# The first four loads of an FNet and SwiGLU kernel, each in two halves of the partitions on two queues

## The chip, the cores and the metric

The kernel runs on one core of a Trainium2 chip. The metric is the device time of one execution in microseconds (us); the kernel before takes 969.46 us, the median of three runs (969.38 to 969.82). A core has TensorE (PE in the profile, with PEld for its weight loads), VectorE (DVE), ScalarE (ACT), GpSimd (POOL) and SyncE (SP), each with an instruction stream of its own, and 16 DMA engines that move data between the chip's main memory and the core's on-chip memory of 128 partitions.

## The reference

`x` has 2048 rows of 640; everything is float32.

```python
xn = _layernorm(x, axis=-1)
# FNet: real part of a DFT over the hidden dim (640) and the sequence (2048)
a = einsum("bsd,ed->bse", xn, dft_hid_re)
b = einsum("bsd,ed->bse", xn, dft_hid_im)
s = einsum("ts,bse->bte", dft_seq_re, a) - einsum("ts,bse->bte", dft_seq_im, b)
# SwiGLU on the same xn
g = silu((silu(xn @ w_gate) * (xn @ w_up)) @ w_down)
return x + s * g
```

## The kernel before

Every float32 product is made of three faster matmuls: an operand is split in a high and a low part (`hl`, by ScalarE and VectorE), and high x high, high x low and low x high are summed in PSUM (`ps`). Products of blocks go by Strassen's seven-product scheme, so VectorE also adds and subtracts blocks. The sequence DFT comes first: for each of four passes `seq(k)` the matrices `cs` (the real and imaginary DFT matrices, cut in 128 x 1024 pieces) are the moving operand and rows of the normalised `x` the weights. Then `hid_s` (hidden DFT), `gate_up` and `down` follow.

All work is recorded first and ordered afterwards. A step of the code calls `pl.prod` (something that has to be ready by a time), `pl.step` (matmuls) or `pl.post`; `schedule` gives each a time, and the list is played back in the order of these times, each operation on its engine's stream. So one line (L82, the recorder) stands in the profile for nearly everything, and the tiles' names tell operations apart: `xn` is `x` and its normalised rows, `raw` any float32 buffer (pieces of `cs` among them), `hl` split operands, `bst`, `mv`, `sm` and `rowst` the statistics of the layer norm.

The change lies in `opening()` (L855), the start of the first pass. It has fixed times around zero: `OPEN_DMA` (L730) lists 16 loads, eight x tiles of 128 rows (one number) and eight pieces of `cs` (two numbers: block and group), issued by SyncE from t = -6 at distances of 0.45. The first four are x tile 0, the first block's first piece of `cs`, x tile 1 and the second block's first piece; the next four are x tiles 2 and 3 and the second pieces. `layer_norm` makes statistics of each x tile on VectorE and takes the root on ScalarE (`AF.Sqrt`, which needs a table loaded). For x tile 0 its result goes straight to TensorE as unsplit float32 weights (`neg`, a `raw` buffer): the first block of three matmuls (two records each in the trace) needs x tile 0 and the first piece of `cs`, the second block the second block's piece. From x tile 1 on the operands are split.

While the first loads are under way, TensorE runs eleven matmuls on a zero tile `z` (`busy`, L633, called at L1380 when the playback passes t = 0). The root's table is loaded at the very start of ScalarE's stream, by a warm-up root on a constant (L1363).

A transfer that SyncE or ScalarE issues tells of its landing by one of eight semaphores (`DMAHW0` to `DMAHW7` in the order below), which are taken in turn over both engines. An issue that takes a semaphore again waits until its transfer before has landed, and SyncE issues strictly in its order.

Of the kernel before, what the change touches and what calls it, by code (L numbers as in the profile page):

```python
# [11 lines left out]
AF = mybir.ActivationFunctionType  # L12
ALU = mybir.AluOpType

P = 128
S, D, F = 2048, 640, 1536
TC = 512
# [261 lines left out]
def tile_fnet_swiglu(  # L279
# [16 lines left out]
    nc = Probe(tc.nc)  # L296
# [5 lines left out]
    pl = Plan()  # L302
    mv = one.tile([P, NS, 2], F32, name="mv")
    sm = one.tile([P, 6, NS], F32, name="sm")
# [10 lines left out]
    def raw(name, a=0, n=None):  # L315
        o, (arena, size) = where[name], pl.size[name]
        n = size - a if n is None else n
        over = arena == "raw" and o >= RAW_KB * 256 - 8
        return space["raw3" if over else arena][:, o + a - over * (RAW_KB * 256 - 8):][:, :n]
# [57 lines left out]
    def wide(ap):  # L377
        return ap.rearrange("p (a b) -> p a b", b=TC)
# [176 lines left out]
    xn = pl.buf(("xn",), "raw2", NS * D)  # L555
# [5 lines left out]
    def xn_tile(k):  # L561
        return space["xn", k // 8][:, k % 8 * D:k % 8 * D + D]

    def load_x(k, lead, eng):
        pl.prod(lead, lambda: eng.dma_start(xn_tile(k), x[k * P:(k + 1) * P, :]), [], [(xn, k)])

    def layer_norm(k0, n, lead, root, stats, small):

# [64 lines left out]
    def busy(bank, n):  # L633

        for _ in range(n):
            nc.tensor.matmul(bank, z[:, :P], z, start=True, stop=True)
# [93 lines left out]
    OPEN_DMA = ((0,), (0, 0), (1,), (1, 0), (2,), (3,), (0, 1), (1, 1), (4,), (5,), (0, 2), (1, 2), (6,), (7,), (0, 3), (1, 3))  # L730
# [11 lines left out]
    def seq(k):  # L742
# [112 lines left out]
        def opening():  # L855
# [3 lines left out]
            at = lambda t: -t  # L859
            part = ((0, b2, dbank[1]), (1, b1, b3[0]))  # L860
# [3 lines left out]
                    seq.n += 1  # L864
                    left[i, g] = pl.buf(("c", seq.n), "raw", 2 * TC)

            def fetch(i, g, t, a=None):
                src = cs[j, i, g // 2, :, 2 * (g % 2):2 * (g % 2) + 2]
                name = left[i, g]
                if a is None:  # L870
                    pl.prod(at(t), lambda: nc.sync.dma_start(wide(raw(name)), src), [], [(name, 0), (name, 1)])
                else:
                    pl.prod(at(t), lambda: nc.sync.dma_start(raw(name, a * TC, TC), src[:, a]), [], [(name, a)])

            t = -6.0
            for what in OPEN_DMA:
                if len(what) == 1:
                    load_x(what[0], at(t), nc.sync)
                else:
                    fetch(what[0], what[1], t, *what[2:])  # L880
                t += 0.45
            neg = [layer_norm(k0, n, [at(x) for x in apply], [at(x) for x in root], [at(x) for x in stats], nc.vector)
                   for k0, n, stats, root, apply in OPEN_LN][0]
# [5 lines left out]
            for (i, kk), (high, low) in OPEN_S.items():  # L889
                name, n = left[i, kk // 2], 1 if kk == 1 else 2  # L890
# [3 lines left out]
            for kk in range(8):  # L894
                for i, banks, db in part if kk < 7 else part[::-1]:
# [6 lines left out]
                    o, a = (s[i, 1], 0) if kk == 1 else (s[i, kk // 2 * 2], kk % 2)  # L902
# [23 lines left out]
        def p2(g):  # L926
            if fresh:
                for kk in (8 + 2 * g, 9 + 2 * g):
                    load_x(kk, 40 + 2 * g, nc.sync)
                layer_norm(8 + 2 * g, 2, *LEAD["xn", 4 + g], nc.gpsimd)  # L930
            return operand("p2", g, load(12, g, 11 if fresh else 20, "raw"))
# [19 lines left out]
        if fresh:  # L951
            opening()
        elif not shared:
            run(("p1", p1, b2, (1, 1)))
# [405 lines left out]
    nc.gpsimd.memset(sm[:, 5, :4], EPS)  # L1360
    nc.gpsimd.memset(sm[:, 5, 4:8], 0.25 * EPS)
    nc.gpsimd.memset(sm[:, 5, 8:], -0.5)
    nc.scalar.activation(sm[:, 0, :1], sm[:, 5, :1], AF.Sqrt)  # L1363
    started = False
    first, last = ExitStack(), ExitStack()
    for i, stack in enumerate((first, last)):
        space["xn", i] = stack.enter_context(tc.tile_pool(name=f"xn{i}", bufs=1)).tile([P, TURN_KB * 256], F32, name=f"xn{i}")
    for i, (t, _, fn, names, _) in enumerate(pl.ops):
        if i == turn:
            last.close()  # L1370
            first.close()
            space["hl2"], space["hl3"] = (stack.enter_context(tc.tile_pool(name=name, bufs=1, reuse_waits="tile")).tile(
                [P, TURN_KB * 256], F32R, name=name) for stack, name in ((ctx, "hl2"), (last, "hl3")))
        if i == back:
            last.close()
            space["raw3"] = ctx.enter_context(tc.tile_pool(name="raw3", bufs=1, reuse_waits="tile")).tile(
                [P, TURN_KB * 256], F32, name="raw3")
        if t >= 0 and not started:
            started = True
            busy(ps[:, 7], 11)  # L1380
        fn()
# [40 lines left out]
```

## Time and profile before

| | us |
|---|---|
| median of 3 runs (lowest to highest) | 969.46 (969.38 to 969.82) |
| the profiled execution | 969.83 |
| its span, first to last instruction | 967.6 |
| TensorE matmuls busy (x4235) | 961.7 |
| VectorE busy (x932) | 734.6 |
| ScalarE busy (x676) | 488.6 |
| GpSimd busy (x184) | 121.3 |

The profile is one execution of the program, taken by the hardware profiler, with times from the first instruction on. A busy share is an average over the whole span; what a change at the start is worth is read from the start. The chain of waits follows the work that ended last back from the end, at each step to what released it. In a timeline, a row gives start, length, engine, instruction and tile (written <- read), a count where like instructions are merged, and in brackets how long the engine stood idle before it and what ended that. "DMA" as a releaser means a landed transfer; SPq rows are the issues in SyncE's queue, merged rows run from the first issue to the end of the last. PE rows of matmuls overlap, since they are pipelined.

### The profile page before, as it was taken

The numbers are of one execution on the slowest core, as the hardware profiler recorded it, in microseconds if no ns is written. First come the engines' busy times: TensorE is split into PE (matmuls) and PEld (weight loads), VectorE is DVE, ScalarE is ACT, GpSimd is POOL, SyncE is SP. The second block draws the span as 40 slices with busy tenths as digits, with TensorE's granted clock in tenths as the row PEclk, the third lists the DMA queues.
The fourth block names the chain that finished last, engine by engine and source line by source line (L and its number), as shares of the span: only waits on it lengthen the run. The fifth ranks groups of instructions, "written<-read, shape, count | busy, mean of one in ns | idle before, by whom it ended". The sixth has DMA issues, their size and how long they took to land.

```text
span 967.6 us, 11521 instructions
## 1 busy us (share of the span) xinstructions
PE 961.7 (99%) x4235; PEld 792.0 (82%) x4235; DVE 734.6 (76%) x932; ACT 488.6 (50%) x676; POOL 121.3 (13%) x184
## 2 busy tenths in 40 slices
PE   9999999999999999999999999999999999999998
PEld 5888888888888888888888888888888888888887
DVE  7889668757774687676987898999978666666775
ACT  5686445454545455544356555563446444444341
POOL 1460211011101110111100211210002000000000
PEclk9999999999999999999999999999999999999999
DMA  9997848494938497778673374439699330105793
GB/s 352 283 249 215 233 147 229 152 271 106 231 109 255 109 236 263 208 196 253 170 213 131 141 265 155 168 136 289 222 292 256 99 133 4 55 1 163 240 346 131
DMA packets 64056, 186.50 MB, mean 193 GB/s; under 512 B 6528, under 2 KB 10368, under 8 KB 64000
## 3 DMA queue, kind: packets, MB, share of 16 engines
q1 hardware_dynamic: 45952, 125.45, 39.0%
q0 software_dynamic: 18048, 60.32, 24.2%
q8 instruction: 33, 0.54, 0.2%
q14 instruction: 23, 0.19, 0.1%
HBM read 151.39 MB, written 34.36 MB: 192 GB/s over the span
## 4 chain that ended last, share of the span: by engine, by line
PE 99%; DMA 0%; DVE 0%; ACT 0%; issue 0%; DVEq 0%; ACTq 0%
PE ps L82 99%; DMA xn<-in_x 0%; DVE raw L82 0%; DVE bst L82 0%; DVE sm L82 0%; ACT raw L82 0%; ACT sm L82 0%; DVE mv L82 0%; DVEq L82 0%; ACTq L82 0%
## 5 line engine op out<-in xcount | busy, mean ns | idle before, releaser
L82 PE MATMUL ps<-hl 128*128 128x512 f32 (+1 forms) x3258 | 780.1, 388 | 0.0
L82 PEld LDWEIGHTS ps<-hl 128*128 128x128 f32 x3258 | 610.1, 188 | 126.6 <-DVE hl L82 0.6
L82 DVE TENSOR_TENSOR hl<-raw,hl 128x1024 fp32r<-128x1024 f32 (+5 forms) x360 | 346.5, 994 | 134.3 <-ACT hl L82 94.4
L82 ACT ACTIVATE hl<-raw 128x1024 fp32r<-128x1024 f32 (+6 forms) x416 | 325.0, 826 | 170.3 <-DVE raw L82 84.8
L82 PE MATMUL ps<-hl,hl 128*128 128x512 f32 (+1 forms) x954 | 259.9, 388 | 0.0
L82 ACT ACTIVATE raw<-ps 128x512 f32<-128x512 f32 (+1 forms) x144 | 97.9, 681 | 231.4 <-PE ps L82 225.2
L82 PEld LDWEIGHTS ps<-hl,hl 128*128 128x128 f32 x954 | 179.0, 188 | 36.9
L82 DVE TENSOR_TENSOR raw<-raw 128x1024 f32<-128x1024 f32 (+7 forms) x216 | 178.6, 849 | 19.8 <-ACT raw L82 15.5
L82 DVE TENSOR_TENSOR raw<-ps,raw 128x512 f32<-128x512 f32 (+1 forms) x95 | 77.2, 814 | 48.4 <-PE ps L82 47.6
L82 DVE TENSOR_TENSOR raw<-raw,raw 128x512 f32<-128x512 f32 (+3 forms) x50 | 44.2, 892 | 6.5 <-ACT raw L82 4.3
L82 ACT ACTIVATE hl<-xn 128x1024 fp32r<-128x1024 f32 (+3 forms) x61 | 42.2, 723 | 13.6 <-PE ps L82 9.1
L82 POOL DMA_DIRECT2D p_dram<-raw x24 | 16.4, 686 | 251.4 <-DVE raw L82 215.7
L82 ACT ACTIVATE raw<-raw 128x512 f32<-128x512 f32 (+1 forms) x30 | 21.5, 718 | 46.7 <-DVE raw L82 46.7
L82 DVE TENSOR_TENSOR hl<-xn,hl 128x1024 fp32r<-128x1024 f32 (+3 forms) x50 | 40.8, 833 | 4.0 <-PE ps L82 3.9
L82 POOL DMA_DIRECT2D raw<-in_cs x36 | 32.5, 984 | 57.7 <-DMA raw<-in_cs 29.1
L82 DVE SCALAR_TENSOR_TENSOR hl<-raw,hl 128x256 fp32r<-128x256 f32 (+4 forms) x56 | 32.7, 586 | 4.0 <-ACT hl L82 4.0
L82 POOL DMA_DIRECT2D out<-raw x10 | 6.9, 689 | 226.6 <-DVE raw L82 197.3
L82 POOL DMA_DIRECT2D d_p<-hl x28 | 15.2, 543 | 71.4 <-ACT hl L82 59.6
L82 ACT ACTIVATE xn<-xn,sm,rowst 128x640 f32<-128x640 f32 (+1 forms) x16 | 14.1, 906 | 5.3 <-DVE sm L82 3.6
L82 DVE BATCH_NORM_STATS2 bst<-xn 128x6 f32<-128x320 f32 x32 | 13.7, 479 | 4.0 <-DMA xn<-in_x 4.0
L82 POOL DMA_DIRECT2D y_dram<-raw x12 | 8.2, 683 | 64.6 <-DVE raw L82 46.2
L82 POOL DMA_DIRECT2D raw<-p_dram x8 | 10.1, 1267 | 44.7 <-DVE raw L82 26.3
(42 smaller groups left out, 84.3 us busy)
## 6 DMA issues: line engine op xcount, KB each, us to landing
raw<-in_cs SPq DMA_DIRECT2D x84, 512.0 KB, 7.0
hl<-d_p SPq DMA_DIRECT2D x56, 384.0 KB, 5.0
raw<-in_cs POOLq DMA_DIRECT2D x36, 512.0 KB, 9.8
raw<-in_wb SPq DMA_DIRECT2D x24, 640.0 KB, 4.7
d_p<-hl POOLq DMA_DIRECT2D x28, 384.0 KB, 4.0
p_dram<-raw POOLq DMA_DIRECT2D x16, 512.0 KB, 4.4
raw<-p_dram SPq DMA_DIRECT2D x8, 768.0 KB, 8.5
xn<-in_x SPq DMA_DIRECT2D x16, 320.0 KB, 9.8
```

Of the source, the lines that this page charges most:

```text
L82: return real(*args, **kw)
```

## The change

`halves` gives, for a load without an engine, the two halves of the partitions with SyncE's queue for the lower 64 and ScalarE's for the upper 64; with an engine it gives one whole load on it. `load_x` and `fetch` use it, and the first four entries of `OPEN_DMA` have no engine. ScalarE's warm-up root, and with it the load of the root's table, is moved from the start of its stream to the point where the playback passes t = -4, behind the first four loads. A branch of `fetch` that was not used is gone.

```diff
+    def halves(eng):
+
+        return ((slice(0, P), eng),) if eng else ((slice(0, P // 2), nc.sync), (slice(P // 2, P), nc.scalar))
+
     def load_x(k, lead, eng):
-        pl.prod(lead, lambda: eng.dma_start(xn_tile(k), x[k * P:(k + 1) * P, :]), [], [(xn, k)])
+        rows = x[k * P:(k + 1) * P, :]
+        for part, queue in halves(eng):
+            pl.prod(lead, lambda part=part, queue=queue: queue.dma_start(xn_tile(k)[part], rows[part]), [], [(xn, k)])
...
-            def fetch(i, g, t, a=None):
+            def fetch(i, g, t, eng):
                 src = cs[j, i, g // 2, :, 2 * (g % 2):2 * (g % 2) + 2]
                 name = left[i, g]
-                if a is None:
-                    pl.prod(at(t), lambda: nc.sync.dma_start(wide(raw(name)), src), [], [(name, 0), (name, 1)])
+                for part, queue in halves(eng):
+                    pl.prod(at(t), lambda part=part, queue=queue: queue.dma_start(wide(raw(name))[part], src[part]),
+                            [], [(name, 0), (name, 1)])
+
+            t = -6.0
+            for n, what in enumerate(OPEN_DMA):
+                eng = nc.sync if n >= 4 else None
+                if len(what) == 1:
+                    load_x(what[0], at(t), eng)
                 else:
...
+                    fetch(*what, t, eng)
                 t += 0.45
...
-    nc.scalar.activation(sm[:, 0, :1], sm[:, 5, :1], AF.Sqrt)
-    started = False
+    started = warm = False
...
+        if t >= -4 and not warm:
+            warm = True
+            nc.scalar.activation(sm[:, 0, :1], sm[:, 5, :1], AF.Sqrt)
```

SyncE's stream at the start of the program, before (the names are written <- read with the shape; `[waits ...]` are the semaphores that an instruction waits for):

```order
L82 DMA xn_108<-in_x 128x640
L82 DMA raw<-in_cs 128x1024
L82 DMA xn_108<-in_x 128x640
L82 DMA raw<-in_cs 128x1024
L82 DMA xn_108<-in_x 128x640 x2
L82 DMA raw<-in_cs 128x1024 x2
L82 DMA xn_108<-in_x 128x640 [waits DMAHW0_49]
L82 DMA xn_108<-in_x 128x640 [waits DMAHW1_49]
L82 DMA raw<-in_cs 128x1024 [waits DMAHW2_49]
L82 DMA raw<-in_cs 128x1024 [waits DMAHW3_49]
L82 DMA xn_108<-in_x 128x640 [waits DMAHW4_49]
```

SyncE's stream at the same place now:

```order
L82 DMA xn_107<-in_x 64x640
L82 DMA raw<-in_cs 64x1024
L82 DMA xn_107<-in_x 64x640
L82 DMA raw<-in_cs 64x1024
L82 DMA xn_107<-in_x 128x640 [waits DMAHW0_49]
L82 DMA xn_107<-in_x 128x640 [waits DMAHW1_49]
L82 DMA raw<-in_cs 128x1024 [waits DMAHW2_49]
L82 DMA raw<-in_cs 128x1024 [waits DMAHW3_49]
L82 DMA xn_107<-in_x 128x640 [waits DMAHW4_49]
L82 DMA xn_107<-in_x 128x640 [waits DMAHW5_49]
L82 DMA raw<-in_cs 128x1024 [waits DMAHW6_49]
L82 DMA raw<-in_cs 128x1024 [waits DMAHW7_49]
```

No load has changed its place; the first four are of 64 partitions, and the waits on landings start at the fifth load where they started at the ninth.

ScalarE's stream at the start of the program, before (`sm<-sm` is the warm-up root, `sm<-mv,sm` the root of x tile 0):

```order
L82 ACT_TABLE_LOAD
L82 ACTIVATE sm<-sm 128x1 [waits Pool_49]
L82 ACTIVATE sm<-mv,sm 128x1 [waits DVE_49,Pool_49]
L82 ACTIVATE hl<-raw 128x512 [waits DMAHW1_49]
L82 ACTIVATE xn_108<-xn_108,sm,rowst 128x512 [waits DMAHW0_49,DVE_49]
```

ScalarE's stream at the same place now:

```order
L82 DMA xn_107<-in_x 64x640
L82 DMA raw<-in_cs 64x1024
L82 DMA xn_107<-in_x 64x640
L82 DMA raw<-in_cs 64x1024
L82 ACT_TABLE_LOAD
L82 ACTIVATE sm<-sm 128x1 [waits Pool_49]
L82 ACTIVATE sm<-mv,sm 128x1 [waits DVE_49,Pool_49]
L82 ACTIVATE hl<-raw 128x512 [waits DMAHW3_49,DMAHW2_49]
L82 ACTIVATE xn_107<-xn_107,sm,rowst 128x512 [waits DMAHW1_49,DMAHW0_49,DVE_49]
```

Four issues have come ahead of the table load, and what reads one of the first four loads waits for two landings, on VectorE and TensorE too. From the fifth load on, the order of the instructions on every engine is that of before.

## Rows read from the trace of the kernel before

**Rows 1.** The chain that ended last: start, length, what (number of instructions).
```profile
0.73 3.01 DMA xn<-in_x
...
3.76 0.90 DVE bst L82 x2
...
4.68 0.22 DVE mv L82
...
4.99 0.30 ACT sm L82
...
6.46 956.86 PE ps L82 x4224
```

**Rows 2.** Waits of PEld, 6.2 to 960 us: us in total, times, longest.
```profile
PEld ps L82 <- DVE raw L82: 1.2, 1, 1.2
PEld ps L82 <- DMA raw<-in_cs: 0.8, 1, 0.8
PEld ps L82 <- DVE hl L82: 0.6, 2, 0.4
PEld ps L82 <- DVE rowst L82: 0.2, 1, 0.2
```

**Rows 3.** Timeline, PE and PEld: start, length, instruction, tile, count, [idle before].
```profile
5.12 0.15 PEld L82 LDWEIGHTS <-z 128*128 128x128 bf16 x1 [0.28 <-issue]
...
8.71 0.59 PE L82 MATMUL ps<-raw,xn 128*128 128x512 f32 x1
9.25 1.12 PE L82 MATMUL ps<-raw 128*128 128x512 f32 x2
...
9.25 0.30 PEld L82 LDWEIGHTS ps<-raw 128*128 128x128 f32 x2 [0.78 <-DMA raw<-in_cs]
...
16.42 0.76 PEld L82 LDWEIGHTS ps<-hl 128*128 128x128 f32 x4 [0.40 <-DVE hl L82]
```

**Rows 4.** Windows: length, busy time (instructions) by engine, PEclk, DMA share, GB/s.
```profile
1.50:2.00 0.50, 0.50 (x2) 0.15 (x1) 0.00 (x0) 0.50 (x1) 0.00 (x0) 1.00 0.63 97
7.00:8.00 1.00, 1.00 (x4) 0.52 (x3) 0.97 (x4) 0.79 (x1) 0.00 (x0) 1.00 0.88 250
12.00:16.00 4.00, 4.00 (x19) 3.29 (x18) 3.54 (x10) 3.63 (x6) 0.19 (x1) 1.00 1.03 418
16.00:20.00 4.00, 4.00 (x18) 2.99 (x18) 3.78 (x11) 1.54 (x3) 0.00 (x0) 1.00 1.03 416
28.00:32.00 4.00, 4.00 (x20) 3.30 (x19) 3.30 (x10) 3.82 (x8) 0.61 (x1) 1.00 1.09 259
```

**Rows 5.** Timeline of ACT, 0 to 9 us.
```profile
0.72 1.28 ACT L82 ACT_TABLE_LOAD   x1 [0.72 <-PEq L1412]
2.02 0.20 ACT L82 ACTIVATE sm<-sm 128x1 f32<-128x1 f32 x1
4.99 0.29 ACT L82 ACTIVATE sm<-mv,sm 128x1 f32<-128x1 f32 x1 [2.77 <-DVE mv L82]
5.26 0.63 ACT L82 ACTIVATE hl<-raw 128x512 fp32r<-128x512 f32 x1
```

**Rows 6.** Timeline of SyncE's queue, 0 to 20 us: issues.
```profile
2.10 0.43 SPq L82 DMA_DIRECT2D raw<-in_cs  x1
2.58 0.91 SPq L82 DMA_DIRECT2D xn<-in_x  x2
...
6.87 2.68 SPq L82 DMA_DIRECT2D raw<-in_cs  x2
```

**Rows 7.** Timeline of DVE, 9 to 17 us.
```profile
9.37 0.69 DVE L82 TENSOR_TENSOR hl<-raw,hl 128x512 fp32r<-128x512 f32 x1
10.25 0.89 DVE L82 BATCH_NORM_STATS2 bst<-xn 128x6 f32<-128x320 f32 x2 [0.20 <-DMA xn<-in_x]
...
15.15 1.22 DVE L82 TENSOR_TENSOR hl<-raw,hl 128x1024 fp32r<-128x1024 f32 x1
```

**Rows 8.** The page, part 5: one group of GpSimd's DMA issues.
```profile
L82 POOL DMA_DIRECT2D raw<-p_dram x8 | 10.1, 1267 | 44.7 <-DVE raw L82 26.3
```

More of the change, by code (lines that the diff above doesn't have):

```diff
@@ L865, in opening @@
                     left[i, g] = pl.buf(("c", seq.n), "raw", 2 * TC)
-            def fetch(i, g, t, a=None):
+            def fetch(i, g, t, eng):
                 src = cs[j, i, g // 2, :, 2 * (g % 2):2 * (g % 2) + 2]
                 name = left[i, g]
-                if a is None:
-                    pl.prod(at(t), lambda: nc.sync.dma_start(wide(raw(name)), src), [], [(name, 0), (name, 1)])
-                else:
[L873 to L880, printed above, removed]
+                for part, queue in halves(eng):
[6 more added lines that the diff above has]
+                    load_x(what[0], at(t), eng)
+                else:
+                    fetch(*what, t, eng)
                 t += 0.45
```

## The prediction

> **What bounds the kernel now.** I read the chain of waits first, then the waits of the weight loads, and only then the first 17 us in time order. The chain goes through the first x tile and some small steps of VectorE and ScalarE to the first real matmul at 6.46, and from there 956.86 us on TensorE alone, of a span of 967.6 [rows 1]. Its weight loads, which start a matmul's work and so show its stalls, wait for other engines and transfers five times between 6.2 and 960 us [rows 2]: 1.2 us for VectorE's `raw` (the first real matmul, at 6.46), 0.8 for a transfer of `in_cs` (at 9.25), two for `hl`, one short one for `rowst`. The longest of the `hl` waits is at 16.42 [rows 3], and no wait comes after it. So from 17 us to the last matmul TensorE runs on without a pause, and whatever the change does to the end, it does by moving the point at which TensorE gets through this opening.
>
> How much is there to win? The eleven warm-up matmuls on `z` step by 0.43 us (a weight load lasts 0.15 and stands 0.28 after the one before; the last is at 5.12 [rows 3], beside the tenth matmul), so the eleventh matmul starts at 5.55 and the array is free at 5.97. The first real matmul starts at 6.46: 0.49 us. The first block's last record starts at 8.71, the next could start 0.43 later, at 9.14, and starts at 9.25: 0.11 [rows 3]. A start after a wait costs 0.10 more: the two records from 9.25 end at 10.37, the second lasts 0.59 like the one at 8.71, so it starts at 9.78, 0.53 after the first where the step is 0.43 [rows 3]. The same holds at 6.46. The stall at 16.42 costs one matmul: 18 are counted in 16 to 20 us, where there are 19 in the 4 us before [rows 4], 0.23. Sum 0.49 + 0.11 + 2 x 0.10 + 0.23 = **1.03 us**. That is all that any speed-up of the opening loads can give, 0.11% of 969.46. What can be told from no change is about 0.2%, or 1.94 us. A gain that can be measured is therefore out, whatever the queues do.
>
> **The change part by part, against the profiled run's own 969.83 us** (its span 967.6 and 2.2 us around it; it lies 0.37 above the median of the three runs, 969.46, so the differences below are put on the median).
>
> The first x tile. Its load is issued at 0.73 and lands 3.01 us later, at 3.74; behind it stand statistics (0.90), aggregate (0.22), square root, four small steps, and the first matmul at 6.46 [rows 1]. The halves are issued at 0.73 by SyncE and at about 0.72 by ScalarE, where ScalarE's first work stood before [rows 5]. There is no issue time to win for this tile, since it was first in its queue already. The transfer engines are 0.63 busy in the half us up to 2.0 [rows 4], so they start at about 1.7, 1 us after the issue. The same bytes in the same 16 engines: 0, if the two queues share an engine as two queues do later. For that I take the stretch 28 to 32 us, where loads of SyncE's and GpSimd's queues run together: the busy share is 1.09 and the rate 259 GB/s, while one queue alone makes 1.03 and 418 at 12 to 16 [rows 4]. Two queues' packets fill an engine's time once, not twice. (GpSimd's are accumulating loads, so the rate itself is no price for ours; the share is.)
>
> A wait more. The statistics now wait for two semaphores. In the chain, an instruction behind one wait starts 0.02 us after its releaser (4.66 to 4.68), one behind two starts at 4.99 after 4.90 [rows 1]: 0.09. So +0.07 at the first matmul, 6.53.
>
> The fourth load, the second block's `cs`. It is issued at 2.10 [rows 6] and reaches TensorE at 9.25 [rows 3]. An engine's queue and not its issue set that: 7 us lie between. The first block, 0.07 later, would end at 9.14 + 0.07 = 9.21, still before 9.25: the 0.07 is absorbed, with 0.04 to spare.
>
> The loads behind the four. Each transfer of the hardware queues takes one of eight semaphores in turn, and an issue waits until the eighth before it has landed. Before, the fifth to eighth load were issued freely, from 2.58 us on [rows 6]. Now eight halves fill all eight, and the fifth (x tile 2) waits for the first half of x tile 0, so for 3.74 by the chain: 1.2 us later than before. It then stands behind what is left of the first four loads. Their last byte arrives at about 9.2, so at 3.74 there are over 5 us of transfers queued in front of it; an issue takes about 1 us to its first packet. It is covered, and x tile 2 reaches VectorE at 10.25 as before [rows 7]. If the cover were gone, it would cost those 1.2 us. The other issues behind it wait for landings at most at 9.2, while some 4 us of loads stand in the queue; from x tile 6 on every issue waits for the same load as before.
>
> Why x tile 2 matters: VectorE ends its earlier work at 9.37 + 0.69 = 10.06 and waits 0.20 us for this tile, then works almost without a break up to 16.37, where the `hl` of the stall at 16.42 is done [rows 7]. So TensorE's last stall hangs on x tile 2's landing, with 0.20 us of slack for all that VectorE does before. The 0.07 of the first step is absorbed here too.
>
> ScalarE's queue and the table. Four issues stand ahead of the table load (1.28 us) and the warm-up root (0.20), which ended at 2.22 before; the first real root starts at 4.99 after 2.77 us of idle time [rows 5]. No trace here shows a DMA issued by ScalarE. From below its price is SyncE's, 0.43 [rows 6]; from above the dearest group of GpSimd's issues, 1.27 [rows 8]. I take SyncE's, the nearest kind, since both issue from a sequencer and GpSimd's DMAs run on its engine. 0.72 + 4 x 0.43 + 1.30 + 0.20 = 3.94, hidden by 1.05 us of idle time. It stays hidden up to (4.99 - 0.72 - 1.50) / 4 = 0.69 us each.
>
> The sum: 0 for the tile, +0.07 absorbed twice, 0 for queue and table: **969.46 + 0.0, 969.5 us**.
>
> **The rivals.** (1) *The halves overlap.* In the opening the engines are busy but slow: 250 GB/s at 7 to 8 us, against 418 at 12 to 16 [rows 4]. If that is a delay per packet which two queues can hide from each other, the first four loads (1.70 MB) take 4.1 us at 418 GB/s from 1.75, and land by 6.2 in place of 9.2; everything in the list above falls away: 969.46 - 1.03 = **968.4**, and half of it 968.9. For it: the slow packets are early only. Against it: the share of 1.09 with two queues.
>
> (2) *The halves don't run side by side.* An engine may serve several transfers of SyncE's queue before it turns to ScalarE's. Then x tile 0 is whole only after first halves of the next two loads. Their landings follow the first by about 1.5 us (the root's successor on ScalarE, which needs `cs`, starts at 5.26 [rows 5]) and 1.6 us (SyncE's issue at 6.87 waits for the third load [rows 6]). Half of the sum is 1.55 us. VectorE's slack takes 0.20, so 16.42 moves by 1.35: **970.8**.
> The Trainium skill, "DMA: Bandwidth & Descriptors", section Queues, rings and completion order, says that an engine goes round the queues a whole packet at a time, of some 9 to 17 descriptors as a rule; by that this rival would come true, if the next loads' descriptors join one packet. The same page's Rules for kernel authors advise against two transfers to disjoint partition halves, because both spread over the same 16 engines; by that the sum stays at 969.5. The share of 1.09 agrees with the second, and no run here shows the first.
>
> (3) *The table comes late*, the one that ends on the slow side. At GpSimd's 1.27 us per issue the warm-up root ends at 0.72 + 5.08 + 1.50 = 7.30, so the first root is 2.3 us late. VectorE's steps up to 10.06 stand behind it in order, so it reaches x tile 2 at 12.4 and not at 10.25, and the stall at 16.42 moves by 2.1: **971.6**, measurably slower. It decides from 0.69 us an issue on. Against it: SyncE's 0.43.
>
> **How the numbers follow.** Forecast, 969.1 to 969.9 (0.4 to either side for the scatter of runs, 0.44 between the lowest and highest of before): 0.63. Rival 1: 0.21. Rival 2: 0.12. Rival 3, or a like delay: 0.04. The range goes from 968.6, so that only the far end of rival 1 is out (0.05), to 970.5, where the upper end of rival 2 (0.04) and rival 3 (0.04) are out: 0.13 in all. By the bound of 0.2%, rivals 1 and 2 are no change either: same 0.63 + 0.19 + 0.11 = 0.93; slower 0.04 + 0.01 from rival 2's tail = 0.05; faster 0.02, the end of rival 1 with a shift in the measurement on top.
>
> **What would show it.** In the changed kernel: the chain's first transfer still about 3.0 us; the first real matmul at 6.4 to 6.6; the weight load's wait for `in_cs` at about 9.25; VectorE's wait for x tile 2 at about 10.25 and the stall at about 16.4; ScalarE's warm-up root done by 4; no wait of TensorE after 17 us. Rival 1 would show as a first transfer under 2.8 us and a rate over 350 GB/s at 5 to 8 us; rival 2 as a first transfer over 4 us; rival 3 as a root that waits for the table and not for VectorE. The forecast is wrong if x tile 2 lands more than 0.4 us away from 10.2, and out of its range only if a new stall of TensorE appears after 17 us.

## The result, and the profile after

The changed kernel takes **971.53 us** (median of 16 runs, 970.77 to 972.70), the kernel before 969.70 beside it (16 runs, 969.38 to 969.90): a ratio of 1.0021, 95% interval 1.0014 to 1.0027. It is slower by 1.83 us (0.19% by the medians, 0.21% by the ratio), clear of noise and outside the range 968.6 to 970.5 that was given.

In the profiled runs (971.29 against 969.83) the span grows from 967.6 to 969.4 us. The head of the page, the span and the busy time of TensorE:

```profile
span 969.4 us, 11533 instructions
...
PE 961.0 (99%) x4235; PEld 791.6 (82%) x4235; DVE 734.6 (76%) x932; ACT 488.7 (50%) x676; POOL 122.1 (13%) x184
```

The same work is done in the same busy time; so the 1.8 us by which the span grows are idle time somewhere. The chain of waits after, from its start (start, length, what), to be held against [rows 1]:

```profile
0.73 0.57 SPq L82
...
1.35 0.84 SPq L82
...
2.25 0.61 SPq L82
...
2.90 7.23 DMA raw<-in_cs
...
10.27 954.05 PE ps L82 x4218
```

Before, the chain went through x tile 0 and reached TensorE at 6.46. Now it goes through four issues of SyncE and the landing of the fourth load at 10.13, and settles on TensorE only at the second block, 10.27 (9.25 before [rows 3]). The fourth issue starts 0.80 us later than before (2.90 for 2.10 [rows 6]), which is most of the 0.92 us that its landing is late (below). That points to the issues; the experiments have to show it.

The waits of PEld from 6.2 us on (in total, times, longest), against [rows 2]:

```profile
PEld ps L82 <- DVE raw L82: 2.2, 1, 2.2
...
PEld ps L82 <- DMA raw<-in_cs: 1.0, 1, 1.0
PEld ps L82 <- DVE hl L82: 0.7, 2, 0.4
PEld ps L82 <- DVE rowst L82: 0.2, 1, 0.2
```

They are the same waits, the first 1.0 us longer. Of that, 0.74 us is the later first real matmul (7.20 for 6.46); the rest is mostly that the warm-up matmuls end earlier in this execution, at 5.46 for 6.18. Behind the stall at 17.43 TensorE runs without a stall in both kernels.

The second place is the end. The timeline around the last matmul, first of the kernel before (SPq is the issue of the last two stores):

```profile
963.03 0.28 PE L82 MATMUL ps<-hl,hl 128*128 128x256 f32 x1
963.30 1.74 SPq L82 DMA_DIRECT2D out<-raw  x2
```

and of the changed one:

```profile
964.03 0.28 PE L82 MATMUL ps<-hl,hl 128*128 128x256 f32 x1
964.31 1.73 SPq L82 DMA_DIRECT2D out<-raw  x2
```

The last matmul starts 1.00 us later. From there to the end of the span it takes 967.6 - 963.03 = 4.6 us before and 969.4 - 964.03 = 5.4 after. So the loss has **two parts: 1.0 us in the opening, 0.8 us behind the last matmul**, where no instruction of the change stands.

The device time is longer than the span, and here the change wins something back: time less span is 2.22 us in the profiled run before and 1.84 in the changed one (1.79 to 1.89 in all 16 of its runs). What stands in it no profile shows. So from the last matmul to the end of the device time it is 6.80 us before and 7.26 after, and the end costs 0.46 us net. With the 1.00 of the opening that is 1.46, the difference of the two profiled runs; the medians lie 0.37 further apart, since the profiled run of before lies 0.13 above its median and that of the changed kernel 0.24 below.

**The opening.** SyncE's queue after (start, length of issue, tiles, count):

```profile
0.73 0.57 SPq L82 DMA_DIRECT2D xn<-in_x  x1
1.35 0.84 SPq L82 DMA_DIRECT2D raw<-in_cs  x1
2.25 0.61 SPq L82 DMA_DIRECT2D xn<-in_x  x1
2.90 0.60 SPq L82 DMA_DIRECT2D raw<-in_cs  x1
3.73 1.11 SPq L82 DMA_DIRECT2D xn<-in_x  x2
```

ScalarE after (ACTq is its queue; in brackets idle time before, and what ended it):

```profile
0.73 0.57 ACTq L82 DMA_DIRECT2D xn<-in_x  x1
...
2.61 0.62 ACTq L82 DMA_DIRECT2D raw<-in_cs  x1
3.26 1.28 ACT L82 ACT_TABLE_LOAD   x1 [3.26 <-issue]
4.55 0.20 ACT L82 ACTIVATE sm<-sm 128x1 f32<-128x1 f32 x1
5.74 0.29 ACT L82 ACTIVATE sm<-mv,sm 128x1 f32<-128x1 f32 x1 [0.99 <-DVE mv L82]
```

A half takes 0.57 to 0.62 us to issue, one 0.84, on either queue, where a whole load took 0.38 to 0.43 ([rows 6] show 0.43). SyncE's fourth issue starts at 2.90 in place of 2.10. The transfers start later too: the first packet in the transfer records is at 1.74 before, and after at 2.08 for ScalarE's half and 2.65 for SyncE's, though both halves are issued at 0.73. The landings of the first four loads, by the trace, before -> whole after (ScalarE's half): x tile 0 3.74 -> 4.41 (3.71), first `cs` 5.24 -> 6.89 (5.72), x tile 1 6.86 -> 8.40 (7.41), second block's `cs` 9.21 -> 10.13 (9.96). Everything behind lands some 0.4 us later, x tile 2 at 10.63 in place of 10.23.

What the transfer engines did meanwhile: two windows of the kernel before (after the length: PE, PEld, DVE, ACT, POOL busy with instructions, PEclk, share of the DMA engines, GB/s),

```profile
1.50:9.00 7.50, 7.22 (x17) 2.42 (x15) 4.05 (x16) 2.72 (x6) 0.37 (x2) 1.00 0.93 287
4.00:5.00 1.00, 1.00 (x4) 0.30 (x2) 0.86 (x3) 0.01 (x1) 0.01 (x1) 1.00 0.91 330
```

and of the changed one:

```profile
1.50:9.00 7.50, 5.76 (x15) 2.12 (x14) 3.23 (x13) 3.22 (x5) 0.18 (x1) 1.00 0.88 246
4.00:5.00 1.00, 1.00 (x5) 0.35 (x3) 0.49 (x2) 0.74 (x2) 0.00 (x0) 1.00 0.77 188
```

At 4 to 5 us the engines are 0.77 busy and move 188 GB/s in place of 330. All eight halves were issued by 3.50, so the length of the issues alone doesn't explain this stretch; what the engines lacked there no row shows. VectorE's stream after shows where the late loads bite:

```profile
4.51 0.89 DVE L82 BATCH_NORM_STATS2 bst<-xn 128x6 f32<-128x320 f32 x2 [4.51 <-DMA xn<-in_x]
...
8.49 0.89 DVE L82 BATCH_NORM_STATS2 bst<-xn 128x6 f32<-128x320 f32 x2 [0.58 <-DMA xn<-in_x]
...
10.79 0.69 DVE L82 TENSOR_TENSOR hl<-raw,hl 128x512 fp32r<-128x512 f32 x1
11.39 0.88 DVE L82 BATCH_NORM_STATS2 bst<-xn 128x6 f32<-128x320 f32 x2
...
16.16 1.22 DVE L82 TENSOR_TENSOR hl<-raw,hl 128x1024 fp32r<-128x1024 f32 x1
```

It now waits 0.58 us for x tile 1, and does x tile 2 at 11.39 without a wait, because it is late itself (it waited for that tile at 10.25 [rows 7]). Its last row here stood at 15.15 [rows 7]: 1.01 later, and with it TensorE's last stall, 16.42 [rows 3] -> 17.43:

```profile
17.43 0.76 PEld L82 LDWEIGHTS ps<-hl 128*128 128x128 f32 x4 [0.42 <-DVE hl L82]
```

The second block, 9.25 -> 10.27, is late by the same.

**The end.** SyncE closes the program by waiting on the eight semaphores of the hardware queues one by one, always from the first to the last, some 0.065 us apart. Where no wait hides it, a pause of some 0.36 us shows among them, between two waits or between the last one and the drain, and its place differs from kernel to kernel. If the last store holds the eighth semaphore, only the drain, and the pause if it falls there, is left when it lands. Four more transfers turn the last store to the fourth: then four waits and the pause come behind its landing. From the closing rows of SyncE in the trace, which the timeline doesn't list, in us (the last column is the device time of the profiled run less the start of the last matmul):

| kernel | last matmul starts | semaphore of the last store | its landing | landing to SyncE's drain | drain to end of span | last matmul to end of time |
|---|---|---|---|---|---|---|
| before | 963.03 | 8th | 966.59 | 0.08 | 0.9 | 6.80 |
| after | 964.03 | 4th | 967.65 | 0.67 | 1.1 | 7.26 |

From the last matmul to the landing it is 3.6 us in both. The waits behind the landing cost 0.6 us more, the barrier of all engines behind the drain 0.2; outside the span 0.4 comes back.

### The profile page after: what moved, and what is told of

It is laid out like the page before. It is cut to its first block, busy times and chain, and to the rows that moved or that the text cites. A ratio compares the mean times of both kernels' runs of the same rounds, so it can differ in the third digit from the quotient of the medians.

```text
span 969.4 us, 11533 instructions
## 1 busy us (share of the span) xinstructions
PE 961.0 (99%) x4235; PEld 791.6 (82%) x4235; DVE 734.6 (76%) x932; ACT 488.7 (50%) x676; POOL 122.1 (13%) x184
## 4 chain that ended last, share of the span: by engine, by line
PE 98%; DMA 1%; SPq 0%; DVE 0%; issue 0%; ACT 0%
PE ps L82 98%; DMA raw<-in_cs 1%; SPq L82 0%; DVE raw L82 0%; ACT raw L82 0%
## 5 line engine op out<-in xcount | busy, mean ns | idle before, releaser
L82 POOL DMA_DIRECT2D raw<-in_xt x6 | 6.9, 1296 | 70.3 <-DVE raw L82 50.7
```

The source lines that it names most:

```text
L82: return real(*args, **kw)
```

## The experiments

The explanations that stood against each other: for the opening, that **two queues get into each other's way** (theory A of the expectations), or that **halves of 64 rows are dear** in themselves (theory B); for the end, the **turn of the eight semaphores** (C); for the spread of the changed kernel's runs, the **gap behind the warm-up matmuls** (D); and, later, that **two queues bring a higher rate** (E). The kernel before beside these runs took 969.72 to 969.76 us.

**Halves on one queue.**

```diff
-        return ((slice(0, P), eng),) if eng else ((slice(0, P // 2), nc.sync), (slice(P // 2, P), nc.scalar))
+        return ((slice(0, P), eng),) if eng else ((slice(0, P // 2), nc.sync), (slice(P // 2, P), nc.sync))
```

> The changed kernel with both halves of each of the four loads issued by SyncE, one behind the other; ScalarE issues nothing, the table load keeps its place. Theory A (two queues that issue at the same time hinder each other's issue, and then run out of step): issues take about 0.4 us again instead of 0.57 to 0.84, the first x tile is whole by 3.8 to 4.1, the second block's cs lands by about 9.3, last matmul at 963.0 to 963.4. Theory B (the halving itself, 64 rows in place of 128, slows the transfers): the second block's cs lands at about 10.1 and the last matmul stays at 964.0. Theory C (the end): eight semaphores in turn, with four more transfers the last store takes the fourth instead of the eighth, and SyncE's closing waits for the others come behind it: the 0.8 us behind the last matmul stay. A with C: 970.3 to 970.7; B with C: 971.5.

Measured: 972.34 us (971.21 to 972.63), ratio 1.0024 (1.0015 to 1.0034). SyncE's queue in it:

```profile
0.73 1.20 SPq L82 DMA_DIRECT2D xn<-in_x  x2
1.98 1.23 SPq L82 DMA_DIRECT2D raw<-in_cs  x2
```

0.6 us for each half, with no second queue beside it; of the whole loads that follow, the first takes 0.59 and the next two 0.43. So the price of the issue belongs to the half, not to the company of ScalarE's queue. The start is another matter: SyncE's first packet comes at 2.10 here and at 2.65 beside ScalarE's half, so of the 0.91 us by which it was late 0.36 belong to the half and 0.55 to the company. The eight issues fill SyncE up to 5.8 us, and the window

```profile
1.50:9.00 7.50, 5.85 (x15) 2.14 (x14) 3.46 (x13) 2.45 (x5) 0.18 (x1) 1.00 0.86 223
```

has the lowest rate of all. The second block's `cs` is whole at 11.35, and the last matmul starts at 964.92, later than either theory had it.

**Whole loads on two queues**, x by SyncE, the first `cs` pieces by ScalarE.

```diff
-                eng = nc.sync if n >= 4 else None
...
-                    load_x(what[0], at(t), eng)
+                    load_x(what[0], at(t), nc.sync)
...
-                    fetch(*what, t, eng)
+                    fetch(*what, t, nc.scalar if what[1] == 0 else nc.sync)
```

> Four whole loads, the two x tiles by SyncE and the two pieces of cs by ScalarE, table behind them; the number of transfers is that of the kernel before. Theory A: the first issues take 0.55 to 0.85 us, the first x tile lands later than 3.74, at about 4.3, and the last matmul comes 0.3 to 1.0 us later than 963.03. Theory B: issues and landings as before, last matmul at 963.0. Theory C: the end as before, 4.6 us from last matmul to the end of the span. A with C: 970.0 to 970.7; B with C: 969.7.

Measured: 972.71 us (971.04 to 973.96), ratio 1.0026 (1.0017 to 1.0036), in two groups: four runs at 971.04 to 971.17, five at 972.67 to 972.82, one at 973.96. The profiled run is one of the lower group. Its issues on ScalarE:

```profile
0.73 0.89 ACTq L82 DMA_DIRECT2D raw<-in_cs  x2
```

Two whole loads in 0.89 us: ScalarE issues a load of 128 rows as cheaply as SyncE does. Its windows:

```profile
1.50:9.00 7.50, 5.81 (x14) 2.04 (x13) 3.21 (x13) 2.75 (x5) 0.18 (x1) 1.00 0.95 313
3.00:4.00 1.00, 1.00 (x4) 0.44 (x3) 0.00 (x0) 0.14 (x1) 0.00 (x0) 1.00 1.01 406
4.00:5.00 1.00, 1.00 (x4) 0.30 (x2) 0.00 (x0) 0.00 (x0) 0.00 (x0) 1.00 1.02 402
```

and, for the second of its rows, the kernel before:

```profile
3.00:4.00 1.00, 1.00 (x4) 0.44 (x3) 0.24 (x1) 0.00 (x0) 0.00 (x0) 1.00 1.02 348
```

The rate rises to 313 GB/s (287 before), from 3 to 4 us to 406 from 348 at the same share of the engines, and yet the kernel is slow, beyond the range of either theory: x tile 0 shares the engines with `cs` from the start and lands at 5.08 in place of 3.74, so the first real matmul comes at 7.79. Here the two queues do harm, by taking from the load that is needed first; it is another harm than the changed kernel's.

**The turn of the semaphores alone**, by four small loads into an unused tile in the middle of the program, where SyncE is idle:

```diff
+        if t >= 560 and not turned:
+            turned = True
+            for n in range(4):
+                nc.sync.dma_start(pad[:, n:n + 1], x[:P, n:n + 1])
```

In the kernel before (this turns its last store from the eighth semaphore to the fourth):

> The kernel before with four loads of one element per partition added at about 560 us, where SyncE's queue has room: the last store takes the fourth semaphore instead of the eighth. Theory C: opening unchanged (last matmul at 963.0), the span ends 0.6 to 0.8 us later, 970.3 to 970.5. Rival (the longer end is chance or belongs to ScalarE's queue being in use): 969.7.

Measured: 969.66 us (969.40 to 969.85), ratio 0.9999 (0.9989 to 1.0008): no difference, against theory C as I had it. In the changed kernel (from the fourth to the eighth):

> The changed kernel with the same four small loads added: twelve... eight more transfers than before in all, so the last store takes the eighth semaphore again. Theory C: last matmul at 964.0 as in the changed kernel, but 4.6 us from there to the end as before: 970.7 to 970.9. Rival: 971.5, the end 5.4 us long.

Measured: 970.75 us (970.25 to 972.15), 0.78 below the 971.53 of the changed kernel; the opening of the profiled run is, with the same loads, 0.39 slower still (second block at 10.54, last matmul at 964.42, 1.39 later than before). So here the end is cured and the opening isn't, and the loss of the opening differs between executions. Later, one small load in the kernel before (from the eighth to the first semaphore):

> The kernel before with one small load at 560 us: the last store takes the first of the eight semaphores, so that eight closing waits come behind its landing instead of none. Theory C: 0.5 us more behind the last landing, 4.9 to 5.4 us from the last matmul to the end instead of 4.58; 970.1 to 970.5. Rival (the end doesn't depend on the turn): 969.7.

Measured: 970.48 us (970.21 to 970.85), 0.73 above before, the lowest run above the highest of before (970.02). The closing rows of all of these, with two kernels from below:

| kernel | last matmul | semaphore | landing | landing to drain | drain to end | last matmul to end of time | time, median |
|---|---|---|---|---|---|---|---|
| before, turned by four | 962.85 | 4th | 966.45 | 0.33 | 0.9 | 6.83 | 969.66 |
| before, turned by one | 962.76 | 1st | 966.36 | 0.87 | 0.9 | 7.51 | 970.48 |
| after, turned by four | 964.42 | 8th | 967.99 | 0.08 | 0.8 | 6.56 | 970.75 |
| halves of columns | 962.57 | 4th, turned to 8th | 966.11 | 0.08 | 0.8 | 6.52 | 969.21 |
| the same, not turned | 962.48 | 4th | 966.03 | 0.67 | 1.1 | 7.19 | 969.72 |

This also says why the first of them cost nothing: the pause of 0.36 us fell ahead of the landing there (at 965.00 to 965.37), so only the 0.25 us of single waits were left, and as much comes back outside the span (time less span is 1.97 us in its runs, 2.22 in those of before). In the changed kernel, in the one turned by one and in the last row the pause stands behind the landing. So the end costs by the semaphore and by the place of the pause; what sets that place stays open. Whole loads on two queues show that the eighth semaphore is no cover by itself: their last store holds it too, and yet 0.39 us lie between its landing (967.49) and the drain, the pause standing there.

**Halves of the columns** in place of halves of the rows, by the same two queues, with the four small loads (so that the last store has the eighth semaphore again):

```diff
-        return ((slice(0, P), eng),) if eng else ((slice(0, P // 2), nc.sync), (slice(P // 2, P), nc.scalar))
+        return ((None, eng),) if eng else ((0, nc.sync), (1, nc.scalar))
+
+    def cut(ap, part, w):
+        return ap if part is None else ap[:, part * w // 2:(part + 1) * w // 2]
...
-            pl.prod(lead, lambda part=part, queue=queue: queue.dma_start(xn_tile(k)[part], rows[part]), [], [(xn, k)])
+            pl.prod(lead, lambda part=part, queue=queue: queue.dma_start(cut(xn_tile(k), part, D), cut(rows, part, D)), [], [(xn, k)])
...
-                    pl.prod(at(t), lambda part=part, queue=queue: queue.dma_start(wide(raw(name))[part], src[part]),
-                            [], [(name, 0), (name, 1)])
+                    pl.prod(at(t), lambda part=part, queue=queue: queue.dma_start(cut(wide(raw(name)), part, 2), cut(src, part, 2)),
+                            [], [(name, 0), (name, 1)] if part is None else [(name, part)])
```

A half of `cs` is then one of its two pieces, and who needs one piece waits for one half alone; this comes with the cut.

> As e4 (the changed kernel with four small loads at 560 us, so that the last store has the eighth semaphore as before), but each of the four loads is cut in halves of its columns, 128 rows each, in place of halves of the partitions. Theory B (a transfer of 64 rows is dear to issue: 0.57 to 0.61 us against 0.38 to 0.45 for one of 128 rows, also alone on one queue in e1, with a first packet 0.35 us later): issues of 0.38 to 0.45 us, first packets 1.0 to 1.2 us after the issue on SyncE's queue, last matmul at 963.0 to 963.5, 969.8 to 970.2. Theory A (two queues out of step are the cost, whatever the shape): first x tile whole at 4.2 or later, last matmul at 964.0 to 964.4, 970.7.

Measured: **969.21 us**, 0.55 below the kernel before beside it (969.76), ratio 0.9994 (0.9985 to 1.0004); the lowest run is 968.86, and apart from one run of 2525.71, left out here, the highest is 970.33. The interval includes a ratio of 1; but eight of the nine other runs lie below the lowest of before (969.51). It is faster than either theory had it. Its queues, SyncE's

```profile
0.73 0.38 SPq L82 DMA_DIRECT2D xn<-in_x  x1
...
2.11 0.43 SPq L82 DMA_DIRECT2D raw<-in_cs  x1
```

and ScalarE's:

```profile
0.73 0.40 ACTq L82 DMA_DIRECT2D xn<-in_x  x1
...
2.13 0.45 ACTq L82 DMA_DIRECT2D raw<-in_cs  x1
```

As many issues, bytes and queues as in the changed kernel, but 128 rows in each, and an issue takes 0.38 to 0.46 us. The window and the first blocks on TensorE:

```profile
1.50:9.00 7.50, 6.79 (x17) 2.56 (x16) 4.09 (x16) 3.52 (x6) 0.37 (x2) 1.00 0.96 309
```

```profile
6.41 1.98 PE L82 MATMUL ps<-raw 128*128 128x512 f32 x4 [0.71 <-DVE raw L82]
8.24 1.02 PE L82 MATMUL ps<-raw,xn 128*128 128x512 f32 x2
9.09 1.88 PE L82 MATMUL ps<-raw 128*128 128x512 f32 x4
```

309 GB/s in place of 246; x tile 0 is whole at 3.87, the second block's `cs` at 8.49, no weight load waits for `in_cs` any more, and the last matmul starts 0.46 us earlier than before, where it started 1.00 later with halves of rows. This is the experiment that settles the opening: the loss came with the 64 rows, not with two halves, two queues or ScalarE's table behind them. The looser waits on `cs` don't explain it, since x tile 0 and `cs` land earlier themselves, and SyncE's first packet is at 1.75, as before the change. Beside the changed kernel with the same four small loads, columns in place of rows are worth 1.54 us (969.21 for 970.75). How the loss divides between the longer issues, the later first packets and the lower rate behind them, the runs don't separate. Without the four small loads:

> e5 (each of the four loads in halves of its columns, on two queues) without the four small loads at 560 us, so that the last store has the fourth of the eight semaphores as in the changed kernel. Theory C (the end: each closing wait that comes behind the last landing costs about 0.065 us, and a stall of 0.36 us in SyncE's closing instructions, hidden before, is laid bare): last matmul at 962.6 as in e5, 4.8 to 5.4 us from there to the end instead of 4.45, 969.5 to 970.0. Rival (the end does not depend on the turn, as e3's times suggest): 969.2, as e5.

Measured: 969.72 us (969.65 to 970.01), ratio 1.0001 (0.9992 to 1.0010). The opening is the same to 0.1 us (second block at 9.01), and what it gains is lost again at the end (the table above). Beside the changed kernel, which has the same semaphores, it is 1.81 us faster. With both halves by SyncE:

```diff
-        return ((None, eng),) if eng else ((0, nc.sync), (1, nc.scalar))
+        return ((None, eng),) if eng else ((0, nc.sync), (1, nc.sync))
```

> e5 with both column halves of each load issued by SyncE, ScalarE issuing nothing. Theory E (in the opening a packet has a delay that two queues hide from each other: 1.5 to 9 us moved 309 GB/s in e5 and 313 in e2 against 287 before): 285 GB/s or less from 1.5 to 9 us, the second block's cs whole at 9.2 or later, 969.8 to 970.4. Rival (smaller packets are what helps): 305 GB/s or more, 969.2 to 969.4.

Measured: 970.50 us (969.63 to 971.04), ratio 1.0007 (0.9998 to 1.0016). Its window:

```profile
1.50:9.00 7.50, 7.21 (x19) 2.77 (x18) 4.39 (x17) 2.63 (x6) 0.38 (x2) 1.00 0.88 239
```

239 GB/s against 309 with the same halves on two queues. Put beside the other windows, both the second queue and the shape count; GB/s from 1.5 to 9 us:

| loads | one queue | two queues |
|---|---|---|
| whole | 287 (before) | 313 |
| halves of rows | 223 | 246 (after) |
| halves of columns | 239 | 309 |

The second queue raises the rate whatever the shape; halves on one queue are slower than whole loads. The first tile is earlier (3.49, first real matmul at 5.81), but the second block's `cs` is whole at 10.11 only, TensorE waits 2.2 us for `hl`, and the last matmul starts at 963.74. This is theory E as far as it goes, with a time at the upper end of its range.

**Only x tile 0 in row halves**, with seven small loads for the semaphores.

```diff
-                eng = nc.sync if n >= 4 else None
+                eng = nc.sync if n >= 1 else None
```

> Only the first x tile in two halves of the partitions on two queues; the other three loads whole by SyncE; seven small loads at 560 us, so that the last store has the eighth semaphore. Theory B: the halves' issues take 0.57 us, their packets start 0.35 us later and the tile is whole at 4.1 to 4.4 (before 3.74), first real matmul at 6.9 to 7.2, but the other three loads land within 0.3 us of before, so TensorE catches up in its waits: last matmul 963.2 to 963.5, 970.0. Theory A: as B for this tile, and the later loads land late too, last matmul at 964.0.

Measured: 970.33 us (969.99 to 971.19), ratio 1.0006 (0.9997 to 1.0016); last matmul at 964.23. SyncE's queue:

```profile
0.73 0.57 SPq L82 DMA_DIRECT2D xn<-in_x  x1
1.36 0.81 SPq L82 DMA_DIRECT2D raw<-in_cs  x1
2.22 0.43 SPq L82 DMA_DIRECT2D xn<-in_x  x1
```

One half costs 0.57, and the whole load behind it 0.81; from the third on it is 0.43 again. From the third load on everything is issued 0.6 us later, and the second block's `cs` lands at 10.59, 1.4 us later than before. Theory B had the other three loads land within 0.3 us of before, and missed: they are 1.3 to 1.7 us late, as theory A had it in kind. The profiled run, 971.03, is near the highest of its runs, so its times are an upper end. One load cut in rows is enough for part of the loss.

**The gap behind the warm-up matmuls.** In the changed kernel TensorE stands for 1.74 us ahead of the first real matmul. More warm-up matmuls should tell whether that is what spreads its runs (15 here, 16 in the kernel with whole loads on two queues):

```diff
-            busy(ps[:, 7], 11)
+            busy(ps[:, 7], 15)
```

> The changed kernel with 15 warm-up matmuls on the zero tile instead of 11; nothing else. Theory D (TensorE now stands idle for up to 2.1 us between warm-up and first real matmul, and in some executions its clock falls back to the lower level for a while, which no single profile has to show; that is why its runs spread over 970.8 to 972.7 and those of before over 0.5 us): with the gap filled the runs above 972 go away, median 971.0 to 971.2. Rival: the spread comes from the landings alone, median 971.5, runs up to 972.5 as before.

Measured: 971.88 us (971.15 to 972.21), ratio 1.0020 (1.0011 to 1.0029): not faster. The warm-up ended at 6.0, and 1.46 us of the gap were left in the profile, so the edit didn't do what it was meant to. In the kernel with whole loads on two queues:

> e2 (four whole loads on two queues) with 16 warm-up matmuls instead of 11. Its ten runs fell in two heaps, four at 971.04 to 971.17 and five at 972.7 to 972.8. Theory D: the upper heap is a clock that fell back in the gap of 1.8 to 2.3 us ahead of the first real matmul; all runs at 971.0 to 971.2. Rival: two heaps again, median 972.7.

Measured: 971.10 us (970.86 to 971.28), ratio 1.0013 (1.0003 to 1.0022): the upper group of the runs is gone, the lower one is where it was. So those 1.6 us seem to go with TensorE's idle time ahead of the first real matmul; but the runs with 11 and with 16 are of two chips and two times, so that a difference between these isn't excluded. The mean granted clock of each run points to the clock: 1.000 in the four lower runs with 11 warm-up matmuls, 0.997 or 0.998 in the five upper ones, and 0.999 or 1.000 in all ten with 16. A mean doesn't say where the lower level stood, though: the profile of the changed kernel with 15 has 0.998 too, and its only stretch at the lower level (0.50, 1.2 GHz) lies from 966.5 us on, behind the last matmul at 964.38. No profile fell into the upper group, so that the clock fell in the gap is likely and not shown.

In the changed kernel the four runs above 972 us have 0.998 as well, but with 15 warm-up matmuls the three above 972 have 0.999 or 1.000. And three profiles with these loads have the second block's `cs` whole at 10.13, 10.40 and 10.66 and the last matmul at 964.03, 964.42 and 964.38, so the landings differ between executions too. Which of the two spreads its runs over 1.9 us stays open.

**How the price goes with the rows**, by eight loads of one element in each of 128, 64, 128, 64, 96, 32, 112 and 16 rows, in the middle of the kernel before (a single run, 970.28 us).

```diff
+            for n, rows in enumerate((128, 64, 128, 64, 96, 32, 112, 16)):
+                nc.sync.dma_start(pad[:rows, n:n + 1], x[:rows, n:n + 1])
```

> The kernel before with eight loads of one element per row at 560 us by SyncE, of 128, 64, 128, 64, 96, 32, 112 and 16 rows; only the lengths of their issues are wanted. Theory B (a row count under 128 is dear): 128 rows 0.33 to 0.43 us, 64 rows 0.50 to 0.60, the others at 0.5 or more too. Rival (dear is only what is issued at the very start of the program): all at 0.33 to 0.43 us.

The group of these issues (ns: least, median, most):

```profile
L82 SPq DMA_DIRECT2D pad<-in_x x8: 420/464/582, 548.5 to 552.3; - x8
```

In order they took 0.45, 0.56, 0.58, 0.48, 0.58, 0.44, 0.42 and 0.43 us: dear ones among 64, 128 and 96 rows, cheap ones among 128, 64 and 16. Neither the theory nor the rival holds: this is no rule by the number of rows. A load behind a half can be dear as well, as in the kernel with one tile cut, and four or seven such loads of 128 rows one behind the other take 0.42 to 0.45 (the small loads of the kernels above), so part of the pattern may be the neighbour's. A single long issue says little: in this run's opening two whole loads took 0.86 and 0.82. But the first issue of a half took 0.55 to 0.57 us in every trace, and that of 128 rows 0.38 to 0.41. The runs don't settle why 64 rows are dear in the opening.

## Why the prediction was wrong, step by step

- **What bounds the kernel, and the cap.** Right. TensorE has no stall after that at 16.42 before and 17.43 after, and all that happens ahead of the last matmul is decided in the opening. The cap of 1.03 us on a gain held: the best opening (halves of columns) gains 0.46. But it is a cap on one side only, and it said nothing of what a worse opening costs.
- **The price of an issue, taken from whole loads.** This is the step that failed first: the sum has 0 for the queue, and the opening lost 1.0 us (1.35 and 1.39 in two other executions with these loads). Four issues on ScalarE's queue were put at 0.43 us, from a load of 128 rows [rows 6], though each is of 64, and SyncE's own were taken as unchanged; they measured 0.57 to 0.62, one 0.84. The bounds of 0.43 and 1.27 held it, but were used for ScalarE's table alone, never for SyncE's own four.
- **x tile 0: "the same bytes in the same 16 engines: 0".** It measured +0.67 at the landing. Its term was bounded by the transfer, not by what comes ahead of it: the first packets are 0.34 us (ScalarE) and 0.91 us (SyncE) late, and no term stood for that. The +0.07 for the second wait was right: statistics start 0.10 us after the landing (4.41 to 4.51), 0.02 before.
- **The fourth load: "an engine's queue and not its issue set that: 7 us lie between".** Wrong. 7 us between issue and use show that a queue stood there, not that it would always be full; at 4 to 5 us the share fell to 0.77. The load is issued 0.80 us later, lands 0.92 us later, and TensorE takes it at 10.27. The slack of 0.04 that was counted there is no cover for that.
- **x tile 2.** Issued at 3.73 as worked out (3.74), and landed 0.40 us later than before, at 10.63, with all that stood in the queue. That is more than 0.4 us from 10.2, the sign that was given for a wrong forecast; yet TensorE does not feel it, since VectorE itself comes to it 1.1 us late (11.39 for 10.25 [rows 7]), held up by x tile 1.
- **ScalarE's table.** Right that it stays hidden, too early by 0.8 us: the warm-up root ends at 4.75 where 3.94, and "by 4" as a sign, had been given, and 0.99 us idle time is left ahead of the real root. The limit of 0.69 us an issue was not reached.
- **The end: "2.2 us around" the span, and what lies between the last matmul and its end, taken as unchanged.** This is the second step that failed. From the last matmul to the end of the span it grew by 0.84 us, what lies around the span fell from 2.22 to 1.84, and the kernel pays 0.46 net, where the sum had 0. The text counted the semaphores in turn for the opening's waits and did not follow the turn to the end of the program. That the forecast would leave its range "only if a new stall of TensorE appears after 17 us" was therefore wrong too. With this part alone the time would have been near 970.2 (an estimate, 969.70 + 0.46), within the range; with the opening's loss and an end 0.24 us shorter than that of before it is 970.75 (the changed kernel, turned). So the opening alone was enough to leave the range.
- **Rival 1, the halves overlap.** (Its 1.75 + 4.1 is 5.9 and not 6.2; nothing rests on that.) True for another cut: two queues reach 309 to 313 GB/s where one has 287, or 239 with two halves in it. The share of 1.09 at 28 to 32 us [rows 4] was the wrong witness: from 3 to 4 us the share is 1.02 with one queue and 1.01 with two, and the rate 348 and 406 GB/s, so the share doesn't tell what two queues bring. The gain of 0.5 us that this rival put at its half is near what the halves of columns have (0.55); that the two agree is in part luck, since 0.46 of it is the opening's.
- **Rival 2, the halves don't run side by side.** Half true. SyncE's half of the first three loads lands 0.70, 1.17 and 0.99 us after ScalarE's; but its sign, a first transfer over 4 us, did not come (3.68, from 0.73 to 4.41), and SyncE's half started late, 2.65 for 2.08. The delay of 1.55 us at x tile 0 that the prediction worked out for two further halves ahead of it did not come either. The Trainium skill, "DMA: Bandwidth & Descriptors" (Queues, rings and completion order), says that an engine takes the queues in turn, a packet at a time; no run here shows the turn itself.
- **Rival 3, the table comes late.** False.
- **The advice** against two transfers to disjoint partition halves (the same page of the Trainium skill, Rules for kernel authors) was read as "costs nothing". It held as advice, and the cost is real: 1.0 us in the opening, by rows cut, while columns cut on the same two queues gained. Another rule in the same section of the Trainium skill, that spreading transfers over several issuing engines doesn't help the bandwidth and saves issue time alone, doesn't agree with the first 9 us here: 309 and 313 GB/s on two queues against 239 and 287 on one, and from 3 to 4 us 406 against 348 with the engines as busy.

## What to carry to other kernels

If an opening load is to be cut over two queues, cut it along the free dimension and keep the 128 rows (that is what gained here, in one kernel), put the halves of the load that is needed first at the head of both queues, and read the issue lengths, the first packets and the rate in that very stretch. A price of an issue is taken from a row of the same shape, or its bounds go into every term that has an issue in it. Where a change alters the number of transfers, follow the turn of the semaphores to the last store: the end of the span moved by up to 0.8 us with it, the device time by 0.5 to 0.7. And read the device time beside the span: what lies between them moved by 0.4 us too.

## What the runs showed that I had not expected

- In the opening a load of 64 rows takes 0.55 to 0.62 us to issue, on SyncE and on ScalarE, alone or beside the other; one of 128 rows with as many bytes (half of the columns) 0.38 to 0.46. A load right behind one of 64 rows can be dear as well (0.81 and 0.84). SyncE's first packet comes at 1.74, alone with a half of rows at 2.10, and beside another such half on ScalarE's queue at 2.65.
- The engines' rate in the first 9 us depends on the number of queues: 239 GB/s for column halves on one, 309 on two; whole loads 287 and 313.
- The closing waits of the program, in fixed order over eight semaphores, with a pause of 0.36 us in a place that differs between kernels: 0.08 to 0.87 us from the last landing to the drain; and time less span, which differs by kernel (some 1.8 to 2.2 us) and hardly by run.
- With five more warm-up matmuls no run was 1.6 us longer any more (whole loads on two queues, on another chip).
